# Attention and MLP interleaved in one pipeline over 384-token tiles

## The chip, the cores and the metric

The kernel runs on one core of one Trainium2 chip. A core has a matrix engine (PE, with its weight loads listed as PEld), a vector engine (DVE), an activation engine (ACT), a general engine (POOL, which also issues DMAs) and a sync engine (SP, which here only issues DMAs). They run side by side, each through its own list of instructions in order, and wait for one another on semaphores. PE multiplies a stationary operand that it has loaded with a moving one and writes to PSUM, which has eight banks of 2 KB per partition; DVE and ACT read PSUM, POOL does not. The metric is the device time in microseconds.

## What is computed

Causal attention for 4 batch entries, 8 heads, 768 positions and head size 64, and behind it an MLP over the 3,072 rows of 512 (8 heads x 64):

```python
scores = scale * np.matmul(q, k.transpose(0, 1, 3, 2))
stream_keep = causal & (is_sink | in_win)   # sink: first 4 keys, window: last 64
mask = np.where(retr[0, :, 0, 0, None, None], full_mask, stream_mask)  # per head
scores = np.where(mask[None, :, :, :], scores, -1000000000.0)
...
a = a / (np.sum(a, axis=-1, keepdims=True) + 1e-09)
return np.matmul(a, v).astype(np.float32)
...
x = np.ascontiguousarray(attn_out.transpose(0, 2, 1, 3)).reshape(B * S, H * D)
h = x @ w_in          # 512 -> 2048
g = h - np.tanh(h)
return (g @ w_out).astype(np.float32)
```

`is_retrieval` is read at run time; a retrieval head sees all earlier keys, a streaming head the sink and the window. Inputs and output are fp32; the products are taken in fp16 with fp32 sums.

## The kernel before

The kernel has two stages, one after the other. A framework gives each engine its list from the program, reordered by its own estimate of when operands are ready; buffers are handed round by tags with a number of buffers each.

**Start.** POOL issues everything that is loaded: q and k of two batch entries in blocks of 128 positions (`load_qk`, lines 84 and 88, 128 KB each), cast from fp32 to fp16 by the DMA, then v (line 96) and the whole of w_in (line 118). Then POOL makes small patterns and DVE writes them into `R01` and `S01` and, for each head, one mask `hmask` over all of its 21 causal blocks (line 188, 128 x 2,688).

**Attention** goes by unit `u`, a pair of heads (`hp`) of one batch entry, 16 units. `emit_transposes` (lines 215 and 219) turns q and k blocks with PE against an identity, and ACT copies them to `qk` (line 223). For each chunk of up to 512 columns PE makes the scores of both heads (`sc`, line 259; each uses 64 of the 128 rows), ACT takes the exp into `pt` (line 267). DVE multiplies the whole `pt` of a head with its mask (line 276). For each of six query blocks PE sums `av` over the key blocks (line 281; v has a column of ones, so column 64 is the row sum), DVE takes the reciprocal (line 289) and scales into `x` (line 290, 64 columns). After the four head pairs of a batch entry PE transposes `x` (line 303) and DVE copies it to `xT` (line 310). PSUM: four banks for `sc`, two for `tp` and `xtp`, two for `av`.

**MLP**, when all of `xT` is there, goes by 8 tiles of 384 rows. For each of 16 blocks `fb` PE sums four matmuls into `ph` (line 328), ACT takes tanh into `th` (line 336), and DVE makes `gt` (line 337). Then, for each 128 rows, PE sums 16 matmuls of 512 columns into `po` (line 344), ACT copies it to `ot` (line 352), and SP stores it. PSUM: four banks for `ph`, two for `po`.

## Time and profile before

| | before |
|---|---|
| median of 3 runs (lowest, highest) | 431.13 us (430.26, 431.20) |
| span of the profiled execution | 429.8 us |
| busy: PE, PEld | 357.2 us, 175.1 us |
| busy: DVE, ACT, POOL | 245.9 us, 209.6 us, 60.5 us |

The span runs from the first to the last instruction of the one execution that was profiled; the runs are timed without a profile, and their median stands 1.3 us above it. In the profile a line such as L281 is the kernel's line 281, an arrow `out<-in` names the tiles, and in the groups the three parts behind it are: count, busy time with the mean of one instruction in ns, and the engine's idle time ahead of them with what ended it. A busy PE is not PE at its peak, since matmuls are pipelined and each one's duration holds its latency.

### The profile page before, as it was taken

The page shows a single profiled execution, that of the slowest core. Times are in us where ns is not written, and L with a number is a line of the kernel's source. Part 1 is how long each engine was busy: PE and PEld are TensorE (multiplying, and loading weights), DVE is VectorE, ACT ScalarE, POOL GpSimd, SP SyncE. Part 2 cuts the span into 40 slices and gives each one's busy share as a digit, 9 for nine tenths or more (in the row PEclk, how much of TensorE's full clock was granted, in tenths as well). Part 3 has the DMA queues.
Part 4 walks back from the last instruction along what each step waited for, and adds up shares of the span by engine and source line. Part 5 has one row for each costly group of instructions (what it writes and reads, how often), then busy time and mean ns, then how long its engine had stood idle before and what let it go on. Part 6 is the DMA issues. An engine that isn't in the chain of part 4 may idle for free.

```text
span 429.8 us, 5768 instructions
## 1 busy us (share of the span) xinstructions
PE 357.2 (83%) x2112; PEld 175.1 (41%) x2112; DVE 245.9 (57%) x676; ACT 209.6 (49%) x505; POOL 60.5 (14%) x71
## 2 busy tenths in 40 slices
PE   1694000888999999999998679999999999999996
PEld 0332000433354334543343335454545454545552
DVE  0005999678767769578767886261707080717160
ACT  1594000666568665776566305262717262635351
POOL 9948801000227011000000000000000000000000
PEclk9999999999999999999999999999999999999999
DMA  9999993800789009000000000101010101020201
GB/s 89 149 142 197 139 67 54 142 2 0 50 34 139 2 2 74 2 0 2 0 2 0 2 0 2 50 26 50 26 49 26 49 24 61 14 75 0 75 0 73
DMA packets 80779, 20.29 MB, mean 47 GB/s; under 512 B 75120, under 2 KB 77168, under 8 KB 80752
## 3 DMA queue, kind: packets, MB, share of 16 engines
q0 software_dynamic: 77152, 13.63, 43.0%
q1 hardware_dynamic: 3600, 6.30, 3.9%
q8 instruction: 16, 0.26, 0.2%
q14 instruction: 11, 0.09, 0.1%
HBM read 27.27 MB, written 6.29 MB: 78 GB/s over the span
## 4 chain that ended last, share of the span: by engine, by line
PE 71%; DVE 15%; POOL 5%; issue 3%; ACT 3%; DMA 3%; POOLq 0%; ACTq 0%
PE ph L328 20%; PE po L344 19%; PE sc L259 14%; PE av L281 11%; DVE hmask L188 4%; DVE pt L276 4%; PE xtp L303 3%; DMA v<-in_v_dram 3%; POOL qraw L84 2%; POOL kraw L88 2%; DVE x L290 2%; PE tp L215 2%; ACT pt L267 2%; DVE xT L310 1%; DVE rinv L289 1%
## 5 line engine op out<-in xcount | busy, mean ns | idle before, releaser
L267 ACT ACTIVATE pt<-sc 128x512 f16<-128x512 f32 (+3 forms) x256 | 103.2, 464 | 75.0 <-PE av L281 46.8
L337 DVE SCALAR_TENSOR_TENSOR gt<-th,ph 128x384 f16<-128x384 f32 x128 | 71.0, 554 | 88.5 <-ACT th L336 77.3
L281 PE MATMUL av<-v,pt 128*128 128x65 f16 x672 | 70.3, 243 | 45.7 <-DVE pt L276 32.5
L259 PE MATMUL sc<-qk 64*128 64x512 f16 (+3 forms) x256 | 92.4, 454 | 5.4 <-ACT pt L267 3.0
L328 PE MATMUL ph<-xT,w_in_t 128*128 128x384 f16 x512 | 86.9, 332 | 0.4 <-DVE xT L310 0.4
L344 PE MATMUL po<-w_out_t,gt 128*128 128x512 f16 x384 | 84.2, 379 | 0.0
L336 ACT ACTIVATE th<-ph 128x384 f32<-128x384 f32 x128 | 62.7, 490 | 39.2 <-PE ph L328 39.2
L281 PEld LDWEIGHTS <-pt 128*128 128x128 f16 x672 | 43.7, 123 | 92.1 <-DVE pt L276 32.8
L328 PEld LDWEIGHTS <-w_in_t 128*128 128x128 f16 x512 | 50.8, 99 | 36.2 <-issue 3.4
L290 DVE TENSOR_SCALAR x<-av,rinv 128x64 f16<-128x64 f32 x192 | 53.2, 281 | 4.3
L344 PEld LDWEIGHTS <-gt 128*128 128x128 f16 x384 | 37.6, 98 | 44.5
L289 DVE RECIPROCAL rinv<-av 128x1 f32<-128x1 f32 x192 | 31.1, 165 | 36.9 <-PE av L281 35.2
L276 DVE TENSOR_TENSOR pt<-pt,hmask 128x2688 f16<-128x2688 f16 x32 | 49.3, 1542 | 0.0
L223 ACT CAST qk<-tp 128x256 f16<-128x256 f32 x96 | 32.9, 382 | 32.0 <-PE tp L219 31.7
L352 ACT ACTIVATE ot<-po 128x512 f32<-128x512 f32 x24 | 14.3, 597 | 69.8 <-PE po L344 69.8
L215 PE MATMUL tp<-ident,qraw 128*128 128x128 f16 x96 | 25.7, 287 | 10.3 <-DMA qraw<-in_q_dram 7.1
L259 PEld LDWEIGHTS <-qk 64*128 64x128 f16 x256 | 19.6, 102 | 29.2 <-issue 17.0
L219 PE MATMUL tp<-ident,kraw 128*128 128x128 f16 x96 | 27.3, 311 | 4.2 <-DMA kraw<-in_k_dram 4.2
L310 DVE CAST xT<-xtp 128x128 f16<-128x128 f32 x96 | 25.3, 285 | 4.6 <-PE xtp L303 3.2
L303 PE MATMUL xtp<-ident,x 128*128 128x128 f16 x96 | 24.1, 278 | 2.5 <-DVE xT L310 1.5
L188 DVE SCALAR_TENSOR_TENSOR hmask<-R,retr_f,S 128x2688 f16<-128x2688 f16 x8 | 23.5, 3015 | 0.0
L84 POOL DMA_DIRECT2D qraw<-in_q_dram x24 | 22.8, 949 | 4.5 <-PE av L281 4.1
(34 smaller groups left out, 88.7 us busy)
## 6 DMA issues: line engine op xcount, KB each, us to landing
out_dram<-ot SPq DMA_DIRECT2D x24, 256.0 KB, 2.0
qraw<-in_q_dram POOLq DMA_DIRECT2D x24, 128.0 KB, 4.7
kraw<-in_k_dram POOLq DMA_DIRECT2D x24, 128.0 KB, 4.7
v<-in_v_dram POOLq DMA_DIRECT2D x4, 768.0 KB, 10.4
w_in_t<-in_moe_w_in_dram POOLq DMA_DIRECT2D x1, 2048.0 KB, 18.3
w_out_t<-in_moe_w_out_dram POOLq DMA_DIRECT2D x1, 2048.0 KB, 14.9
retr_i<-in_is_retrieval_dram SPq DMA_DIRECT2D x1, 8.0 KB, 2.5
```

The lines of the kernel that those rows point to most:

```text
L188: nc.vector.scalar_tensor_tensor(out=hmask[h][:], in0=R01[:], scalar=retr_f[:, 2 * h : 2 * h + 1], in1=S01[:], op0=ALU.mult, op1=ALU.add,)
L259: nc.tensor.matmul(out=pscs[hh][:, 0:cw], lhsT=qk[lo : lo + 64, S + jb * 128 : S + jb * 128 + 128], rhs=qk[lo : lo + 64, jb * 128 + c0 : j ...
L267: nc.scalar.activation(out=pts[hh][:, OFF[jb] + c0 : OFF[jb] + c0 + cw], in_=pscs[hh][:, 0:cw], func=AF.Exp, scale=inv_sqrt_d,)
L276: nc.vector.tensor_mul(out=pt[:], in0=pt[:], in1=hmask[h][:])
L281: nc.tensor.matmul(out=pav[:, 0 : D + 1], lhsT=pt[:, c0 : c0 + 128], rhs=v1[:, h, jb, :], start=(jb == 0), stop=(jb == qb),)
L289: nc.vector.reciprocal(out=rinv[:], in_=pav[:, D : D + 1])
L290: nc.vector.tensor_scalar(out=xts[b][qb][:, h * D : h * D + D], in0=pav[:, 0:D], scalar1=rinv[:], scalar2=XS, op0=ALU.mult, op1=ALU.mult,)
L303: nc.tensor.matmul(out=px[:], lhsT=xts[b][qb][:, cb * 128 : cb * 128 + 128], rhs=ident16[:], start=True, stop=True,)
L328: nc.tensor.matmul(out=ph[:], lhsT=w_in_t[:, cb, fb * 128 : fb * 128 + 128], rhs=xT[cb][:, tt * TTN : tt * TTN + TTN], start=(cb == 0), st ...
L336: nc.scalar.activation(out=th[:], in_=ph[:], func=AF.Tanh, scale=1.0 / XS)
L337: nc.vector.scalar_tensor_tensor(out=gt[:, fb, :], in0=th[:], scalar=-XS, in1=ph[:], op0=ALU.mult, op1=ALU.add,)
L344: nc.tensor.matmul(out=po[:], lhsT=gt[:, fb, tsub * 128 : tsub * 128 + 128], rhs=w_out_t[:, fb, :], start=(fb == 0), stop=(fb == NFB - 1),)
```

## The change

The kernel is written anew around 8 tiles of 384 positions, two per batch entry: `t` is the tile, `c = t % 2` its half. In the first half (even tiles) a head has 6 causal blocks, in the second (odd) 15. Line numbers of the new program stand in the rows below.

- **Loads.** SP loads q and k of a tile in fp32, each partition taking three neighbouring positions of a head (768 bytes), `load_qk`. `cast_qk` makes fp16 copies: on DVE for tiles 0 and 1, on POOL for the others. v comes in blocks of 128 positions, w_in and w_out in four parts each, all by POOL.
- **Transposes** (`st_T`): six per tile and head pair into one PSUM bank in fp16, and one DVE copy of 768 elements to `qkT`, which puts positions back in order. ACT has no part in it.
- **Scores and exp** (`st_S`): blocks are packed into groups of up to 512 columns per head, both heads in one PSUM tile of two banks, one exp for both.
- **Masks.** Only the diagonal block and the one before it are multiplied with a mask, `m4` (512 columns per head). Blocks farther away have no mask: they use `vf`, copies of v and its ones column multiplied with the head's flag (1 or 0) by POOL, `far_v`; in block 0 the sink rows keep theirs.
- **av** (`st_A`): all three query blocks and both heads of a tile in one PSUM bank, one reciprocal and one multiply of 384 elements. The scale 4,096 sits in the ones column as 1/4,096. `st_X` transposes the result into the same bank tag `m` (one bank), and one DVE copy makes `xT`.
- **Pipeline.** The program has 128 steps, one for each `fb` of the 8 tiles. A step is `H_unit` (the `ph` sum, tanh and `gt` of tile `t`), pieces of a later tile's attention by a table `plan`, and three `po` matmuls of tile `t - 1` (`O_mms`). Tile 0's attention stands ahead of the steps, tile 1's lies in steps 0 to 15, an even tile's later on in 9 steps and an odd one's in 23; steps 112 to 127 have none. Behind the steps come the 48 `po` matmuls of the last tile.
- **PSUM**: two tiles of two banks for `sc` and the transposes, one bank `m`, two for `ph` (`h`), one for `po` (`o`).

On DVE, at the start of the program, the rows before are (`R`, `sdiag`, `soff` are parts of the masks):

```order
L127 CAST retr_f<-retr_i 128x16
L106 CAST ident_90<-ident_85 128x128
L171 CAST R_144<-causal 128x128
L160 TENSOR_TENSOR sdiag<-causal,winlo 128x128
L162 TENSOR_TENSOR tmpm<-winlo,sinkrows 128x128
L166 TENSOR_TENSOR soff_162<-offwin,sinkrows 128x128
L164 TENSOR_TENSOR sdiag_160<-causal,tmpm 128x128
L171 CAST R_144<-causal 128x128 x5
```

And now, at the same place (`raw_q`, `raw_k` are the fp32 tiles, 97 and 99 of tile 0, 163 and 165 of tile 1; `t_q`, `t_k` their fp16 copies):

```order
L201 CAST t_q_149<-raw_q_97 128x1536
L201 CAST t_k_151<-raw_k_99 128x1536
L155 TENSOR_SCALAR nz<-retr_i 128x16
L160 TENSOR_TENSOR rflag<-nz 128x8
L201 CAST t_q_360<-raw_q_163 128x1536
L128 CAST ident_111<-ident_106 128x128
L201 CAST t_k_362<-raw_k_165 128x1536
L225 COPY qkT_0_175<-tp_176 128x2x3x128
L162 TENSOR_TENSOR rflag_134<-rflag,sinkrows 128x8
L168 TENSOR_TENSOR tmpm<-winlo,sinkrows 128x128
```

The casts of both tiles, and with them the wait for four loads, have moved ahead of the first copy of transposed q and k and of the masks.

On ACT, in the middle of attention, the rows before are (`pt_2156` and `pt_2157` belong to the two heads of a pair):

```order
L267 ACTIVATE pt_2156<-sc_2182 128x512
L267 ACTIVATE pt_2157<-sc_2183 128x512
L267 ACTIVATE pt_2156<-sc_2188 128x384
L267 ACTIVATE pt_2157<-sc_2189 128x384
L267 ACTIVATE pt_2156<-sc_2194 128x256
L267 ACTIVATE pt_2157<-sc_2195 128x256
```

And now, in the steps of tile 1 and the first of tile 2 (`th` is the tanh of a step, the number behind it `fb`; `ot` the eviction of `po`):

```order
L269 ACTIVATE pt_1171<-sc_2_1230 128x2x512
L269 ACTIVATE pt_1171<-sc_3_1235 128x2x384
L346 ACTIVATE th_12_1245<-ph_12_1240 128x384
L346 ACTIVATE th_13_1272<-ph_13_1267 128x384
L346 ACTIVATE th_14_1291<-ph_14_1286 128x384
L346 ACTIVATE th_15_1312<-ph_15_1307 128x384
L363 ACTIVATE ot_2_1318<-po_2_1198 128x512
L346 ACTIVATE th_0_1329<-ph_0_1324 128x384
L269 ACTIVATE pt_1336<-sc_0_1337 128x2x512
L269 ACTIVATE pt_1336<-sc_1_1342 128x2x512
L346 ACTIVATE th_1_1355<-ph_1_1350 128x384
```

The MLP's tanh and evictions have moved from behind all exps to between them, so that a tanh can now stand behind two exps of both heads.

The diff, cut to its core:

```diff
-        qraw = load_pool.tile([128, NSB, H, D], FP16, tag="qraw", name="qraw")
-        kraw = load_pool.tile([128, NSB, H, D], FP16, tag="kraw", name="kraw")
...
+    raw_pool = pool("raw", 4)
+    t16_pool = pool("t16", 2)
...
+    pt_pool = pool("pt", 3)
...
+    def load_qk(t):
+        b, c = divmod(t, 2)
+        for nm, src in (("q", q), ("k", k)):
+            r = raw_pool.tile([128, H, NB, D], FP32, tag="raw", name=f"raw_{nm}{t}")
+            nc.sync.dma_start(
+                out=r[:].rearrange("p h i d -> p h (i d)"),
+                in_=src[b, :, c * TT : (c + 1) * TT, :].rearrange(
+                    "h (p i) d -> p h (i d)", i=NB
+                ),
+            )
...
+    def mask_head(h):
+        nc.vector.scalar_tensor_tensor(
+            out=m4[:, h, :], in0=D4[:].rearrange("p a c -> p (a c)"),
+            scalar=rflag[:, h : h + 1], in1=S4[:].rearrange("p a c -> p (a c)"),
+            op0=ALU.mult, op1=ALU.add,
+        )
...
-        nc.vector.scalar_tensor_tensor(
-                out=hmask[h][:], in0=R01[:], scalar=retr_f[:, 2 * h : 2 * h + 1],
...
+    def far_v(t):
+        b, c = divmod(t, 2)
+        parts = ((0, 1, rflag0), (1, 3, rflag)) if c == 0 else ((3, 4, rflag),)
+        for lo, hi, fl in parts:
+            nc.gpsimd.tensor_mul(
+                out=vfs[b][:, :, lo:hi, :],
+                in0=v1s[b][:, :, lo:hi, :],
+                in1=fl[:].unsqueeze(2).unsqueeze(3).to_broadcast([128, H, hi - lo, D + 1]),
+            )
...
+    def cast_qk(t, eng):
+        for nm in ("q", "k"):
+            c16 = t16_pool.tile([128, NB, H, D], FP16, tag=f"t16{nm}", name=f"t16_{nm}{t}")
+            eng.tensor_copy(
+                out=c16[:], in_=raws[nm, t][:].rearrange("p h i d -> p i h d")
+            )
...
+        tp = bank([128, 2, NB, 128], FP16, "sc", 2, f"tp{n}")
+        for g, nm in enumerate(("q", "k")):
+            for i in range(NB):
+                nc.tensor.transpose(
+                    out=tp[:, g, i, :], in_=t16s[nm, t][:, i, 2 * hp : 2 * hp + 2, :],
+                    identity=ident16[:],
+                )
+        nc.vector.tensor_copy(
+            out=qkT[b, hp][:, :, c * TT : (c + 1) * TT].rearrange("x g (p i) -> x g i p", i=NB),
+            in_=tp[:],
+        )
...
+    GROUPS = {
+        0: [[(0, 0, 2), (1, 1, 2)], [(2, 2, 1), (0, 2, 1)]],
+        1: [[(3, 3, 2), (4, 4, 2)], [(5, 5, 1), (2, 3, 3)], [(0, 3, 3), (3, 5, 1)], [(1, 3, 3)]],
+    }
...
+            sc = bank([128, 2, 512], FP32, "sc", 2, f"sc{n}_{gi}")
+            o = 0
+            for jb, q0, nb in GROUPS[c][gi]:
+                for hh in range(2):
+                    lo = 64 * hh
+                    nc.tensor.matmul(
+                        out=sc[:, hh, o : o + nb * 128],
+                        lhsT=qk[lo : lo + 64, 1, jb * 128 : jb * 128 + 128],
+                        rhs=qk[lo : lo + 64, 0, q0 * 128 : (q0 + nb) * 128],
+                        start=True, stop=True,
+                    )
...
+            nc.scalar.activation(
+                out=pts[n][:, :, o0 : o0 + w], in_=sc[:, :, 0:w], func=AF.Exp, scale=inv_sqrt_d
+            )
...
-            nc.vector.tensor_mul(out=pt[:], in0=pt[:], in1=hmask[h][:])
+        if g0 == 0:
+            pt = pts[n]
+            hs = slice(2 * hp, 2 * hp + 2)
+            if c == 0:
+                nc.vector.tensor_mul(out=pt[:, :, 0:512], in0=pt[:, :, 0:512], in1=m4[:, hs, :])
+                nc.vector.tensor_mul(
+                    out=pt[:, :, 512:640], in0=pt[:, :, 512:640], in1=m4[:, hs, 256:384]
+                )
+            else:
+                pv = pt[:, :, 0:768].rearrange("p a (r c) -> p a r c", r=3)
+                nc.vector.tensor_mul(
+                    out=pv, in0=pv,
+                    in1=m4[:, hs, 256:512].unsqueeze(2).to_broadcast([128, 2, 3, 256]),
...
+            avs[n] = bank([128, NB, 2, D + 1], FP32, "m", 1, f"av{n}")
...
+                    vv = v1s[b] if jb >= qb - 1 else vfs[b]
+                    co = COL[c][jb, qb]
+                    nc.tensor.matmul(
+                        out=av[:, i, hh, :], lhsT=pts[n][:, hh, co : co + 128],
+                        rhs=vv[:, h, jb, :], start=(x == 0), stop=(x == len(order) - 1),
+                    )
...
-                rinv = sm_pool.tile([128, 1], FP32, tag="rinv")
...
+            rinv = sm_pool.tile([128, NB, 2], FP32, tag="rinv", name=f"rinv{n}")
+            nc.vector.reciprocal(out=rinv[:], in_=av[:, :, :, D])
+            x16 = x_pool.tile([128, NB, 2, D], FP16, tag="x16", name=f"x16_{n}")
+            nc.vector.tensor_mul(
+                out=x16[:], in0=av[:, :, :, 0:D],
+                in1=rinv[:].unsqueeze(3).to_broadcast([128, NB, 2, D]),
+            )
...
+        xp = bank([128, NB, 128], FP16, "m", 1, f"xp{n}")
+        for i in range(NB):
+            nc.tensor.transpose(
+                out=xp[:, i, :], in_=x16s[n][:, i, :, :], identity=ident16[:]
+            )
+        nc.vector.tensor_copy(out=xTs[t][:, hp, :], in_=xp[:].rearrange("p i c -> p (i c)"))
...
-    ps_h = ctx.enter_context(tc.tile_pool(name="ps_h", bufs=4, space=bass.MemoryType.PSUM))
-    ps_o = ctx.enter_context(tc.tile_pool(name="ps_o", bufs=2, space=bass.MemoryType.PSUM))
...
+        ph = bank([128, TT], FP32, "h", 2, f"ph{t}_{fb}")
...
+                pos[t] = bank([128, DM], FP32, "o", 1, f"po{t}_{ts}")
...
+        qa = [lambda: st_A(n, (0, 1), False), lambda: st_A(n, (2,), True)]
+        qs = quanta_S(nS) if nS is not None else []
+        res = []
+        while qs or qa:
+            if qs:
+                res.append(qs.pop(0))
+            if qa:
+                res.append(qa.pop(0))
+        if nT is not None:
+            res.append(lambda: st_T(nT))
+        res.append(lambda: st_X(n))
+        return res
+
...
+    NU = NTT * HP
+    cast_qk(0, nc.vector)
+    for h in range(H):
+        mask_head(h)
+    far_v(0)
+    load_qk(1)
+    load_v(1)
+    ones_v(1)
+    for j in (2, 3):
+        load_w_in(j)
+    st_T(0)
+    st_T(1)
...
+    def span(t):
+        if t == 1:
+            return 0.0, 16.0
+        lo = 16.0 * (2 * ((t - 2) // 2) + 1)
+        return (lo, lo + 9.0) if t % 2 == 0 else (lo + 9.0, lo + 32.0)
...
+    for t in range(1, NTT):
+        lo, hi = span(t)
+        fs = []
+        for hp in range(HP):
+            n = t * HP + hp
+            if first:
+                fs += [lambda: st_T(HP), lambda: st_T(HP + 1)] + quanta_S(HP)
+                first = False
+            if hp == 0 and t + 1 < NTT:
+                fs.append(lambda t=t: load_qk(t + 1))
+                fs.append(lambda t=t: (load_v(t + 1), ones_v(t + 1)))
+            if hp == 1 and t + 1 < NTT:
+                fs.append(lambda t=t: cast_qk(t + 1, nc.gpsimd))
+                fs.append(lambda t=t: far_v(t + 1))
+            fs += slot(n, n + 1 if n + 1 < NU else None, n + 2 if n + 2 < NU else None)
+        for i, f in enumerate(fs):
+            put(int(lo + (hi - lo) * i / len(fs)), f)
+
...
+    for t in range(NTT):
+        for fb in range(NFB):
+            s = t * NFB + fb
+            fs = plan.get(s, [])
+            half = (len(fs) + 1) // 2
+            for f in fs[:half]:
+                f()
+            H_unit(t, fb)
+            for f in fs[half:]:
+                f()
+            if t:
+                O_mms(t - 1, 3 * fb, 3 * fb + 3)
...
+    O_mms(NTT - 1, 0, NB * NFB)
```

More of the change, by code (lines that the diff above doesn't have):

```diff
@@ L92, in load_qk, with ones_v, load_w_in @@
-        loads[b] = (qraw, kraw)
-    def load_v(b):
-        v1 = v_pool.tile([128, H, NSB, D + 1], FP16, tag="v1", name="v1")
+                out=v1s[b][:, :, i, 0:D],
+                in_=v[b, :, i * 128 : (i + 1) * 128, :].rearrange("h p d -> p h d"),
+            )
+    def ones_v(t):
+        b, c = divmod(t, 2)
+        nc.gpsimd.memset(v1s[b][:, :, c * NB : (c + 1) * NB, D : D + 1], 1.0 / XS)
+    w_in_t = []
+    w_out_t = []
+    def load_w_in(j):
+        w = w_pool.tile([128, HP, 512], FP16, tag=f"win{j}", name=f"win{j}")
```

431 lines of the change are left out of this document (176 added, 255 removed).

## The prediction, made before the changed kernel had run

> **What bounds the kernel now.** I read the busy table by stretch first, then the chain of work that ended last, the groups of instructions by shape, the waits, and the timeline at the seams. The stretches (columns: length, then PE, weight loads, DVE, ACT, POOL busy):
>
> ```profile
> 0.00:40.00 40.00, 23.18 (x108) 9.93 (x108) 3.75 (x12) 23.89 (x69) 31.19 (x41) 1.00 1.85 143
> 40.00:70.00 30.00, 0.00 (x0) 0.00 (x0) 29.93 (x26) 0.00 (x0) 13.44 (x15) 1.00 1.38 90
> 70.00:257.00 187.00, 165.39 (x1108) 76.83 (x1109) 141.19 (x512) 108.68 (x284) 15.87 (x17) 1.00 0.38 29
> 257.00:425.80 168.80, 168.65 (x896) 88.31 (x895) 71.00 (x129) 76.45 (x151) 0.00 (x0) 1.00 0.10 37
> ```
>
> Three limits follow one another: 70 us of start, in which PE stands still from 40 to 70 while DVE builds masks; 187 us of attention; 169 us of MLP with PE full and DVE and ACT half idle.
>
> ```profile
> 1.36 1.00 POOL qraw L84
> ...
> 22.63 10.89 DMA v<-in_v_dram
> ...
> 53.91 14.73 DVE hmask L188 x5
> ...
> 257.08 12.97 PE ph L328 x64
> 270.05 10.36 PE po L344 x48
> 280.41 10.40 PE ph L328 x64
> ...
> 425.82 0.60 ACT ot L352
> ```
>
> The chain's start runs over POOL, which issues 24 loads of q and k, then v, then the masks' first steps behind them, and DVE's `hmask` last. In the MLP a `ph` matmul takes 10.40/64 = 0.1625 us, a `po` 10.36/48 = 0.216. The first tile's `ph` took 2.57 longer, in its first 16 matmuls:
>
> ```profile
> 257.08 5.17 PE L328 MATMUL ph<-xT,w_in_t 128*128 128x384 f16 x16 [0.38 <-DVE xT L310]
> ```
>
> That is 0.323 each, twice 0.1625: PE had come out of attention at half speed. The clock column reads 1.00 everywhere, so only durations show it. The groups by shape agree, 512 columns take 598 ns in attention (L259) and 379 in the MLP (L344):
>
> ```profile
> L344 PE MATMUL po<-w_out_t,gt 128*128 128x512 f16 x384 | 84.2, 379 | 0.0
> L337 DVE SCALAR_TENSOR_TENSOR gt<-th,ph 128x384 f16<-128x384 f32 x128 | 71.0, 554 | 88.5 <-ACT th L336 77.3
> L281 PE MATMUL av<-v,pt 128*128 128x65 f16 x672 | 70.3, 243 | 45.7 <-DVE pt L276 32.5 <-DVE x L290 12.4
> L336 ACT ACTIVATE th<-ph 128x384 f32<-128x384 f32 x128 | 62.7, 490 | 39.2 <-PE ph L328 39.2
> L267 ACT ACTIVATE pt<-sc 128x512 f16<-128x512 f32 x96 | 57.0, 612 | 56.9 <-PE av L281 46.8 <-DVE x L290 5.4 <-PE sc L259 4.0
> L290 DVE TENSOR_SCALAR x<-av,rinv 128x64 f16<-128x64 f32 x192 | 53.2, 281 | 4.3
> L259 PE MATMUL sc<-qk 64*128 64x512 f16 x96 | 51.5, 598 | 2.3 <-ACT pt L267 1.1 <-ACT qk L223 0.5
> ...
> L276 DVE TENSOR_TENSOR pt<-pt,hmask 128x2688 f16<-128x2688 f16 x32 | 49.3, 1542 | 0.0
> ...
> L289 DVE RECIPROCAL rinv<-av 128x1 f32<-128x1 f32 x192 | 31.1, 165 | 36.9 <-PE av L281 35.2
> ...
> L310 DVE CAST xT<-xtp 128x128 f16<-128x128 f32 x96 | 25.3, 285 | 4.6 <-PE xtp L303 3.2
> ...
> L188 DVE SCALAR_TENSOR_TENSOR hmask<-R,retr_f,S 128x2688 f16<-128x2688 f16 x8 | 23.5, 3015 | 0.0
> ...
> L267 ACT ACTIVATE pt<-sc 128x128 f16<-128x128 f32 x64 | 17.4, 296 | 5.9 <-PE sc L259 5.5
> ...
> L352 ACT ACTIVATE ot<-po 128x512 f32<-128x512 f32 x24 | 14.3, 597 | 69.8 <-PE po L344 69.8
> ```
>
> PE's weight loads in attention wait for DVE's many small evictions of `av`:
>
> ```profile
> PE av L281 <- DVE pt L276: 32.5, 1, 32.5
> ...
> PEld L281 <- DVE x L290: 30.2, 64, 3.1
> ...
> PEld L281 <- DVE rinv L289: 18.5, 55, 0.9
> ```
>
> **The change, part by part.**
>
> *DVE and ACT prices.* ACT: (612-296)/3 = 105 ns per 128 columns, so 1,024 columns take 1.03 us and 768 take 0.82. A head pair of an even ("light") tile has exps of 1,024 and 512: 1.65 us; of an odd ("heavy") tile three of 1,024 and one of 768: 3.92. DVE from PSUM: (554-285)/256 = 1.05 ns per element, so the `qkT` copy of 768 elements takes 0.96; `x16` and `xT` (384) 0.55 each by L337, the reciprocal 0.17 by L289. Masks by L276: 1,280 elements for a light pair (in two instructions: 0.73 in proportion, 1.06 if each adds L289's 165 ns as a fixed part; I take 0.9), 1,536 for a heavy one (0.88 to 1.05; 0.95). So DVE pays 3.13 for a light and 3.18 for a heavy pair, 6.3 for what took it 159/16 = 9.9 (L276, L289, L290, L310 over 16 head pairs of a whole batch entry), the `qkT` copies that it takes from ACT included.
>
> *PE prices.* Four transposes follow in 0.29 us, eleven `av` matmuls in 0.79, and two 512-column score matmuls of a head pair in 0.73, 0.13 apart, side by side:
>
> ```profile
> 22.93 0.29 PE L215 MATMUL tp<-ident,qraw 128*128 128x128 f16 x1
> ...
> 23.22 0.31 PE L219 MATMUL tp<-ident,kraw 128*128 128x128 f16 x1
> ```
>
> ```profile
> 158.39 0.79 PE L281 MATMUL av<-v,pt 128*128 128x65 f16 x11
> ```
>
> ```profile
> 149.92 0.73 PE L259 MATMUL sc<-qk 64*128 64x512 f16 x2
> ```
>
> At half speed a transpose costs 0.10, an `av` (0.79-0.24)/10 = 0.055 (the last one's own 0.24 is L281's mean), a score pair 0.84 ns a column (0.323/384). At full speed: transpose 0.05, score pair 0.42 ns; `av`, never seen there, between 0.027 and 0.055, I take 0.04. Light pair: 9 transposes, 768 paired columns, 12 `av` = 0.45+0.33+0.48 = 1.26 us (half speed 2.2). Heavy: 0.45+0.81+1.20 = 2.46 (4.15). Not side by side, scores add 0.33 and 0.81. A step is one H unit (4 x 0.1625) and three `po` (3 x 0.216): 1.30 us.
>
> *A, start.* POOL's 24 q,k issues and the 23.5 us of `hmask` go; m4 costs 8 x 3.015 x 512/2,688 = 4.6, say 5.2 with fixed parts. What is late next is q,k itself, in fp32 on SP's queue, beside v and w_in on POOL's:
>
> ```profile
> q0 software_dynamic: 77152, 13.63, 43.0%
> q1 hardware_dynamic: 3600, 6.30, 3.9%
> ...
> retr_i<-in_is_retrieval_dram SPq DMA_DIRECT2D x1, 8.0 KB, 2.5
> ```
>
> A packet took 0.43 x 16 x 429.8/77,152 = 38 ns (256 B read) or 75 ns (mean 1.75 KB). A tensor of one tile is 1,024 packets of 768 B, between those: 2.4 to 4.8 us. In DVE's order the casts of tile 1 stand ahead of the first `qkT` copy, so four tensors must land: 10 to 19 us, 3 more for the issue and the 2.5 of latency that `retr_i` shows, and up to 8 where v's 3 x 1,024 packets of 38 ns come between on the same 16 engines; 13 to 30, taken 20. Then cast 1.3 (0.85 to 1.7, at half or all of 1.05 ns), two copies 1.9, ten small ones 2.5, m4 5.2, masks 0.9: first `av` at 32, against
>
> ```profile
> 70.17 0.35 PE L281 MATMUL av<-v,pt 128*128 128x65 f16 x3 [32.54 <-DVE pt L276]
> ```
>
> Tile 0's four pairs then run one behind the other through the single bank `m`: `av` 0.9, reciprocal 0.2, a `qkT` copy 0.96 and a mask 0.9 between, `x16` 0.55, transposes 0.55, `xT` 0.55 = 4.6. MLP starts at 32+18 = **50** (it was 257).
>
> *B, steps 0 to 15* (H of tile 0, heavy tile 1, no `po` due): PE 16 x 0.65 + 4 x 2.46 = 20 at full speed, 37 at half; ACT 16 x 0.49 + 15.7 = 23.5; DVE 16 x 0.554 + 12.7 = 21.6. PE begins at half speed, is then full, and should rise: **28** (24 to 37).
>
> *C, steps 16 to 111*, three times a light tile over 9 steps and a heavy one over 23. PE 32 x 1.30 + 4 x 1.26 + 4 x 2.46 = 56.5 (x3 = 169); DVE 32 x 0.554 + 25.2 = 43 (129); ACT 32 x 0.49 + 22.3 + 6 x 0.6 = 41.6 (125). So MLP work covers nearly all of attention's DVE and ACT time. Not covered, by my estimate: a light tile's 9 steps hold 9 x 0.554 + 4 x 3.13 = 17.5 of DVE against 9 x 1.30 + 4 x 1.26 = 16.7 of PE, about 3 with hand-overs (x3 = 9). A tanh behind two exps gives its `h` bank back after 0.33 + 2.06 + 0.49 + 0.55 = 3.4, while PE has two `po` groups, an H unit and 18 `av` to do, 3.0: 0.4 per heavy pair (x12 = 5). The single `o` bank comes back after 0.4 of latency and 0.6 of eviction, behind 0.65 of H: 0.3 x 18 = 5. **188**, with 170 if all is hidden.
>
> *D, steps 112 to 127*: 16 x 1.30 + 3 x 0.45 = **22**. *E, the last 48 `po`*: 10.4, two bank waits of 1.1, and the 4.0 us that now lie between 425.82 and the span's end: **16.6**.
>
> Out-stores, w_in, w_out and v cost nothing: their queues stand nearly idle after 70 us, and POOL's 32 issues of about 1.0 us (the chain's first row) fall in 250 us. If q,k or a cast came late, a tile's 9 or 23 steps stand ahead of it; with that cover gone, the next `qkT` copy waits on DVE, and with it the `gt` behind it and PE's `h` banks. The flag-scaled copies of V take the far blocks out of DVE's mask multiplies (2,688 elements per head and batch fall to 1,408) and put `far_v` on POOL, which is busy 16 of 187 us there: at nothing, while DVE has its slack; without it, the second rival.
>
> Sum 50+28+188+22+16.6 = 304.6 of span. The profiled span is 429.8, the median 431.13, so 1.3 lie around it: **306 us**.
>
> **Rivals.**
>
> That MLP and attention are not interleaved at all is excluded by ACT's order above.
>
> *The clock stays low (slower than before).* Speaks for it: 187 us of attention, PE 88% busy by the table, never rose. Against: there PE waited for `av` evictions; here it is short of time in B at half speed (37 against 23.5). If it held through B and C: C = 3 x (32 x 2.59 + 4 x 2.2 + 4 x 4.15) = 325, total 306+137+9 = 452. It decides the sign from (431-306-9)/137 = 85% of C on; half of C gives 384. The Trainium skill ("TensorE: Matmul & The Clock Gate", "A second HAM failure mode: psum-queue depth-cycling") has this as a rule against such a change: a PE that cycles through PSUM banks with short idle gaps swings between both clocks. By that rule, the half-and-half time is the one to expect; the attention rows bear out the low clock, no row a swing.
>
> *DVE and POOL block each other.*
>
> ```profile
> 37.24 2.33 POOL L169 MEMSET S<- 128x2688 f16 x1
> ...
> 37.77 2.72 DVE L171 CAST R<-causal 128x128 f16<-128x128 f32 x5
> ```
>
> Five casts of 128 elements, 0.7 us in all at 1.05 ns an element, took 2.72: they began beside the memset and ended after it. A cast of 1,536 elements at the memset's 0.87 ns would take 1.3 us, say 1.5 with a read. If each of POOL's 17 operations in C (10 casts, 7 `far_v`) held DVE so long where DVE is the limit, C grows by 25: 331. Against: heavy stretches have 14 us of DVE slack each.
>
> *Everything hides*: `av` at 0.027 (pairs of 1.10 and 2.07, C at 163), the first `av` at 25: 306-25-7 = 274.
>
> **Chances.** Forecast 0.60 (288 to 325); low clock through C 0.04 (452), in a part of it 0.10 (330 to 430); DVE held 0.14 (325 to 346); all hidden 0.12 (270 to 288). The range 278 to 346 leaves out about 0.2. Faster by over 0.2% (what can be told from no change) 0.95; within 0.01; slower 0.04.
>
> **What would show it.** `ph` at 326 to 332 ns and `po` at 379 from about 60 us on (524 and 600: low clock); first `av` near 32; `ph` from 50; PE idle under 25 us in C, ended by DVE `gt` and `xT`; POOL casts beside stretched mask multiplies. Wrong if PE idles over 15% of C, or if the casts of tile 1 come after 30.

## The result, and the profile after

The changed kernel takes **310.14 us** (median; runs of 309.1 to 310.9) against 431.16 beside it on the same chip: ratio 0.720, 95% interval 0.718 to 0.721. The profiled execution took 309.1 and spans 307.4. Here and below a median takes in every run of a kernel, while a ratio leaves out a run more than 1.5% above the kernel's fastest (there was one in e_maskall and one in e_nat).

The busy table by stretch, cut at the first `av`, the fifth `ph` matmul (the first on the third head pair's `xT`), the starts of steps 16 and 112, and the end of the last `ph` (columns as before: length, then PE, weight loads, DVE, ACT, POOL busy, the clock, DMA):

```profile
0.00:34.29 34.29, 4.07 (x35) 2.80 (x35) 19.74 (x29) 4.31 (x5) 13.35 (x24) 1.00 1.19 236
34.29:49.22 14.93, 10.18 (x104) 6.68 (x105) 11.78 (x20) 4.47 (x6) 8.49 (x10) 0.99 1.28 204
49.22:79.93 30.71, 28.50 (x294) 15.71 (x292) 22.75 (x40) 21.83 (x33) 14.73 (x15) 0.89 0.87 139
79.93:268.34 188.41, 175.52 (x1623) 98.19 (x1622) 124.35 (x225) 112.32 (x183) 29.31 (x27) 1.00 0.25 49
268.34:289.37 21.03, 20.76 (x111) 10.73 (x110) 8.86 (x16) 8.91 (x19) 0.00 (x0) 1.00 0.10 38
289.37:307.40 18.03, 11.49 (x51) 4.78 (x49) 0.55 (x1) 2.88 (x5) 0.00 (x0) 1.00 0.15 59
```

Where the kernel before had 187 us of attention and then 169 of MLP, there is now one stretch of 188 in which PE works 175.5 and DVE and ACT 124 and 112. PE's idle time there is 12.9 us (188.4 less 175.5). The groups of that stretch (80 to 268) say what ended it; behind the last bar stand a group's idle time and what ended it:

```profile
L341 PE MATMUL ph<-xT,win 128*128 128x384 f16 x384 | 80.5, 326 | 0.5 <-DVE gt L347 0.5
L356 PE MATMUL po<-wout,gt 128*128 128x512 f16 x276 | 77.8, 379 | 1.8 <-ACT ot L363 1.8
L259 PE MATMUL sc<-qkT 64*128 64x128 f16 (+2 forms) x252 | 20.1, 268 | 5.9 <-DVE qkT L225 5.2 <-ACT pt L269 0.7
L324 PE MATMUL xp<-ident,x 128*128 128x128 f16 x72 | 8.0, 220 | 4.4 <-DVE x L311 4.3
```

`ph` and `po` have the durations of full speed. The clock row of the page shows one dip, in the seventh and eighth slice (a fall to half from 48.9 to 55.7 us); ahead of 45 us nothing is recorded, and durations there are those of half speed:

```profile
PEclk9999996899999999999999999999999999999999
```

The page's chain by line, and the two copies from PSUM among DVE's groups:

```profile
PE po L356 20%; PE ph L341 18%; DVE qkT L225 11%; PE sc L259 7%; ACT pt L269 6%; DMA raw_k<-in_k_dram 5%; PE av L303 4%; DVE gt L347 3%; DVE pt L276 3%; DVE x L311 3%; DVE pt L277 2%; ACT th L346 2%; ACT ot L363 2%; PE tp L221 2%; DVE m L180 1%
```

```profile
L225 DVE COPY qkT<-tp 128x768 f16<-128x768 f16 x32 | 45.9, 1434 | 1.4 <-PE tp L221 1.3
...
L327 DVE COPY xT<-xp 128x384 f16<-128x384 f16 x32 | 10.9, 342 | 2.0 <-PE xp L324 2.0
```

The largest line that is not PE's is the `qkT` copy: 11% of the chain, 1.43 us each. The copy of half as many elements, L327, takes a quarter of that.

The start, in DVE's timeline (time, length, what):

```profile
5.81 1.75 DVE L201 CAST t_q<-raw_q 128x1536 f16<-128x1536 f32 x1 [5.81 <-DMA raw_q<-in_q_dram]
8.50 1.75 DVE L201 CAST t_k<-raw_k 128x1536 f16<-128x1536 f32 x1 [0.94 <-DMA raw_k<-in_k_dram]
...
13.88 1.75 DVE L201 CAST t_q<-raw_q 128x1536 f16<-128x1536 f32 x1 [3.33 <-DMA raw_q<-in_q_dram]
15.54 0.22 DVE L128 CAST ident<-ident 128x128 f16<-128x128 f32 x1
20.20 1.75 DVE L201 CAST t_k<-raw_k 128x1536 f16<-128x1536 f32 x1 [4.43 <-DMA raw_k<-in_k_dram]
21.86 1.42 DVE L225 COPY qkT<-tp 128x768 f16<-128x768 f16 x1
```

Tile 0's q and k were cast by 10.25, but the identity (made at 5.4) stood behind tile 1's q, and the first `qkT` copy behind tile 1's k, for which DVE waited 4.43 us.

### The profile page after: what moved, and what is told of

It is laid out like the page before. It is cut to its first block, busy times and chain, and to the rows that moved or that the text cites. A ratio compares the mean times of both kernels' runs of the same rounds, so it can differ in the third digit from the quotient of the medians.

```text
span 307.4 us, 5361 instructions
## 1 busy us (share of the span) xinstructions
PE 250.5 (81%) x2208; PEld 138.9 (45%) x2208; DVE 188.0 (61%) x329; ACT 154.7 (50%) x249; POOL 65.9 (21%) x75
## 4 chain that ended last, share of the span: by engine, by line
PE 51%; DVE 26%; ACT 10%; DMA 5%; issue 5%; SPq 1%; ACTq 0%
PE po L356 20%; PE ph L341 18%; DVE qkT L225 11%; PE sc L259 7%; ACT pt L269 6%; DMA raw_k<-in_k_dram 5%; PE av L303 4%; DVE gt L347 3%; DVE pt L276 3%; DVE x L311 3%; DVE pt L277 2%; ACT th L346 2%; ACT ot L363 2%; PE tp L221 2%; DVE m L180 1%
## 5 line engine op out<-in xcount | busy, mean ns | idle before, releaser
L269 ACT ACTIVATE pt<-sc 128x1024 f16<-128x1024 f32 x96 | 82.8, 918 | 64.1 <-PE sc L259 63.8
L341 PE MATMUL ph<-xT,win 128*128 128x384 f16 x512 | 109.3, 331 | 0.5 <-DVE gt L347 0.5
L356 PE MATMUL po<-wout,gt 128*128 128x512 f16 x384 | 105.3, 379 | 4.2 <-ACT ot L363 4.0
L347 DVE SCALAR_TENSOR_TENSOR gt<-th,ph 128x384 f16<-128x384 f32 x128 | 69.1, 546 | 51.3 <-ACT th L346 51.0
L341 PEld LDWEIGHTS <-win 128*128 128x128 f16 x512 | 45.1, 99 | 30.8 <-issue 6.5
L259 PE MATMUL sc<-qkT 64*128 64x128 f16 (+2 forms) x352 | 32.0, 282 | 22.8 <-DVE qkT L225 15.0
L225 DVE COPY qkT<-tp 128x768 f16<-128x768 f16 x32 | 45.9, 1434 | 1.4 <-PE tp L221 1.3
L303 PEld LDWEIGHTS <-pt 128*128 128x128 f16 x672 | 29.0, 100 | 14.6 <-DVE pt L276 3.3
L259 PEld LDWEIGHTS <-qkT 64*128 64x128 f16 x352 | 14.4, 96 | 46.7 <-DVE qkT L225 19.2
L303 PE MATMUL av<-v,pt 128*128 128x65 f16 x352 | 28.8, 199 | 3.3 <-DVE pt L276 3.0
L95 POOL DMA_DIRECT2D v<-in_v_dram x24 | 21.7, 919 | 18.3 <-PE av L303 17.5
L303 PE MATMUL av<-vf,pt 128*128 128x65 f16 x320 | 24.0, 196 | 0.2
L311 DVE TENSOR_TENSOR x<-av,rinv 128x384 f16<-128x384 f32 x32 | 17.7, 552 | 0.7
## 6 DMA issues: line engine op xcount, KB each, us to landing
win<-in_moe_w_in_dram POOLq DMA_DIRECT2D x4, 512.0 KB, 14.6
```

The costliest lines, as they stand in the source:

```text
L95: nc.gpsimd.dma_start(out=v1s[b][:, :, i, 0:D], in_=v[b, :, i * 128 : (i + 1) * 128, :].rearrange("h p d -> p h d"),)
L225: nc.vector.tensor_copy(out=qkT[b, hp][:, :, c * TT : (c + 1) * TT].rearrange("x g (p i) -> x g i p", i=NB), in_=tp[:],)
L259: nc.tensor.matmul(out=sc[:, hh, o : o + nb * 128], lhsT=qk[lo : lo + 64, 1, jb * 128 : jb * 128 + 128], rhs=qk[lo : lo + 64, 0, q0 * 128 ...
L269: nc.scalar.activation(out=pts[n][:, :, o0 : o0 + w], in_=sc[:, :, 0:w], func=AF.Exp, scale=inv_sqrt_d)
L303: nc.tensor.matmul(out=av[:, i, hh, :], lhsT=pts[n][:, hh, co : co + 128], rhs=vv[:, h, jb, :], start=(x == 0), stop=(x == len(order) - 1),)
L311: nc.vector.tensor_mul(out=x16[:], in0=av[:, :, :, 0:D], in1=rinv[:].unsqueeze(3).to_broadcast([128, NB, 2, D]),)
```

## The experiments

All times are medians; ratios are to the kernel before, run beside them. Stage marks (us in the profiled span) of all kernels, worked out from the starts of the matmuls:

| kernel | time | ratio (95%) | first `av` | fifth `ph` | step 16 | step 112 | end of span |
|---|---|---|---|---|---|---|---|
| changed kernel | 310.14 | 0.718–0.721 | 34.3 | 49.2 | 79.9 | 268.3 | 307.4 |
| e_serial | 390.88 | 0.902–0.909 | 32.4 | 203.4 | 221.0 | 347.1 | 386.2 |
| e_start | 300.03 | 0.694–0.697 | 24.5 | 39.8 | 71.2 | 258.6 | 297.7 |
| e_readstride | 299.72 | 0.693–0.702 | 34.4 | 46.7 | 77.4 | 258.9 | 297.9 |
| e_contig | 295.13 | 0.681–0.687 | 33.0 | 42.9 | 69.1 | 253.7 | 292.8 |
| e_span | 300.24 | 0.696–0.701 | 36.4 | 50.5 | 79.4 | 259.0 | 298.0 |
| e_actcast | 307.68 | 0.712–0.718 | 36.5 | 48.7 | 80.4 | 268.1 | 307.1 |
| e_maskall | 309.89 | 0.717–0.723 | 33.2 | 49.1 | 81.2 | 268.6 | 307.6 |
| e_dmacast | 297.58 | 0.688–0.696 | 24.2 | 39.6 | 68.9 | 258.8 | 297.4 |
| e_obank | 308.10 | 0.714–0.719 | 35.9 | 50.6 | 81.0 | 270.4 | 306.3 |
| e_nat | 283.88 | 0.653–0.662 | – | – | – | – | – |
| b_full | 278.46 | 0.645–0.651 | 15.5 | 29.7 | 62.7 | 241.3 | 276.8 |
| b_two | 285.82 | 0.663–0.667 | 15.4 | 29.1 | 70.8 | 247.9 | 283.5 |

For e_serial the fifth column gives the first `ph`, which there comes behind all of attention. e_nat's profiled execution took 287.08, 3.2 us more than its median, so its marks are left out. Kernels with the same start differ at the first `av` by 2 us and more (34.3 to 36.5; 32.4 in e_serial), so a difference of 2 us between two rows' marks alone says little.

### Each part of the change undone

**e_serial**, the interleaving:

```diff
-            put(int(lo + (hi - lo) * i / len(fs)), f)
+            f()                       # attention of all tiles at once
...
+    with tc.issue_after(last attention transpose):
     for t in range(NTT):              # then the MLP of all tiles
```

> All of the changed kernel's attention runs first and its MLP after it (every H matmul is queued behind the last attention transpose; xT gets 8 buffers, ot 2). Theory (the MLP's PE work hides attention, and that is the larger part of the gain): attention alone is a chain through DVE, ACT and the single bank m. Tile 0's pairs followed each other every 4.6 us in the changed kernel (xT at 37.91, 42.49); at 4.6 for a light and 5.0 for a heavy pair 32 pairs take 154 from 34 on, the MLP then 169 plus 4.5 of tail, so 355 to 372 us, ph begins at about 190, and PE stays at half speed through attention. Rival (the lighter attention is the gain, interleaving adds little): pairs at DVE's own 3.5 and ACT's 3.9 make 118, MLP from 152, 322 to 330 us, with the clock up during attention.

It took 390.88: slower than either theory gave, on the side of the first. Attention ran from 32.4 to 203.4, pairs of heavy tiles 5.5 us apart (`x` at 188.66, 194.12, 199.63) where 5.0 was expected, and the MLP took 183 more, where the kernel before needed 173. PE at work and waiting, by stretch, the clock (no record stands ahead of 72 us, and durations there are those of half speed), and PE's largest wait over the whole run (us in all, times, longest):

```profile
32.42:203.40 170.98, 116.98 (x1279) 74.72 (x1280) 107.52 (x172) 80.79 (x92) 52.17 (x51) 0.70 0.50 74
203.40:368.14 164.74, 162.29 (x848) 83.32 (x847) 70.72 (x128) 72.27 (x147) 0.00 (x0) 0.98 0.09 33
```

```profile
PEclk9999999955656555655796999999999999999999
```

```profile
PE sc L260 <- DVE qkT L226: 48.0, 31, 5.7
```

So the 121 us of the change part into 40 (431 to 391) for everything else in it, and 81 (391 to 310) for interleaving. The 40 are nearly all the start: the first `av` moved from 70.17 to 32.4. The lighter attention by itself won 16 us (187 to 171), of which the MLP gave back 10. Lighter steps do little in a chain in which each engine waits for the next; what they did was to fit under the MLP. Of PE's 54 us of idle time in that stretch (171 less 117), 43.5 were score matmuls waiting for the `qkT` copy, which stands behind the reciprocal and `x16` in DVE's list. So the 81 us hold for this program with its stepped copy and its one bank `m`; a version with attention first that has a faster copy, or that gives attention the banks of the MLP, was not run, and might leave interleaving less to win.

**e_maskall**, the flag-scaled copies of V:

```diff
-                    vv = v1s[b] if jb >= qb - 1 else vfs[b]
+                    vv = v1s[b]
...
+                    nc.vector.tensor_scalar(   # far blocks, per head and flag
+                        out=pts[n][:, hh, lo:hi], in0=pts[n][:, hh, lo:hi],
+                        scalar1=fl[:, h : h + 1], scalar2=None, op0=ALU.mult,
+                    )
```

> The flag-scaled copies of V go; DVE multiplies the far key blocks by the head's flag in place (two instructions per light pair, six per heavy pair). By the multiplies' 0.28 us for 256 and 0.68 for 1,024 elements that is 0.42 us more per light and 2.1 more per heavy pair: 40 us more on DVE, and POOL's 12 multiplies of 1.05 to 2.0 go. Theory (in the heavy stretches DVE has 17 of 41 us free, so only the light tiles and tile 1 pay): 311 to 316 us. Rival 1 (the copies are what keeps DVE off the limit): 322 or more. Rival 2 (POOL's multiplies cost as much as they save, in the start and beside the masks): 305 to 309.

309.89, the same as with the copies. DVE's group of the new multiplies:

```profile
L299 DVE TENSOR_SCALAR pt<-pt,rflag 128x256 f16<-128x256 f16 (+3 forms) x128 | 33.8, 313 | 8.1 <-ACT pt L274 7.5
```

33.8 us more on DVE, and no time: heavy stretches grew (steps 25 to 48 from 41.4 to 43.4, 57 to 80 from 41.4 to 43.0), light ones shrank (48 to 57 from 24.2 to 20.7). In steps 48 to 57 of the changed kernel three mask multiplies had been stretched by 3.1 us beside POOL's `far_v`, which is gone here. Under the interleaving this part of the change is worth nothing measurable. The time lies between the first theory's range and the second rival's. The theory had the place wrong, since it let the heavy stretches go free and the light ones pay; the rival's mechanism shows.

**e_dmacast**, the fp32 loads with casts on chip (here undone, so that the DMA casts again):

```diff
-            nc.sync.dma_start(out=r[:].rearrange(...), in_=...)   # fp32, 768 B
+            for i in range(NB):
+                nc.gpsimd.dma_start(out=r[:, i, :, :], in_=...)   # to fp16, 256 B
```

> q and k come as fp16 by casting DMAs on POOL's queue, three per tensor and tile in 256-byte reads, and the sixteen casts on DVE and POOL go; positions are placed as in the changed kernel. Theory (fp32 loads on SP's queue buy the start): 6 x 1,024 packets of 38 ns on 16 engines take 15 us, v comes behind them on the same queue, first av at 34 to 42, and POOL's 36 more issues are hidden later while 17 us of its casts go: 308 to 320 us. Rival (the casts and the wait for tile 1's tensors cost more than small packets): first av under 32, 298 to 307.

297.58: the rival, and more. This part of the change **cost** 12.6 us. The 15 us that I had given to the small packets were too many: transposes began at 10.94, released by the identity, with all of tile 0's q and k there, and the first `av` stood at 24.2 instead of 34.3. From step 16 to 112 both kernels take about the same (190.0 and 188.4), so it is the start that differs, and the next kernel says by what.

**e_start**: the loads and casts stay; tile 1's casts are queued later.

```diff
-    cast_qk(1, nc.vector)
+    with tc.issue_after(xmul[1].ins):     # x16 of tile 0's second pair
+        cast_qk(1, nc.vector)
```

> Tile 1's two casts are queued on DVE behind the x16 of tile 0's second pair; nothing else is touched. Theory (the start waits in DVE's order for data that tile 0 does not need): ident is cast at 10.4 instead of 15.5, the first qkT copy stands at 11 instead of 21.9, the first av comes at 22 to 24 instead of 34.3, and 3.5 us come back as the casts now stand between tile 0's pairs: 300 to 304 us. Rival (the transfers set the start: v landed at 14.3, far_v follows on POOL and slows DVE, and the loads collide): first av at 29 or later, 306 to 311 us.

300.03, as the theory had it. The first `av`:

```profile
24.49 0.51 PE L304 MATMUL av<-v,pt 128*128 128x65 f16 x6 [4.64 <-DVE pt L277]
```

10 of the 12.6 us of the fp32 loads were the place of two casts in DVE's list, ahead of work that did not need them.

### The terms of the sum

**e_readstride** and **e_contig**, the `qkT` copy. The copy puts positions 3p+i in order, so it writes 2-byte elements 6 bytes apart.

```diff
-            out=qkT[...].rearrange("x g (p i) -> x g i p", i=NB), in_=tp[:],
+            out=qkT[...].rearrange("x g (p i) -> x g p i", i=NB),      # e_readstride
+            in_=tp[:].rearrange("x g i p -> x g p i"),
+            out=qkT[...], in_=tp[:].rearrange("x g i p -> x g (i p)"), # e_contig
```

> The qkT copy walks its elements in the order of the destination: it reads PSUM in steps and writes SBUF in order. Theory (the 1,434 ns are the 6-byte steps of 2-byte writes, and a copy in order goes at xT's 342 ns for 384): 0.62 to 0.75 us a copy, 32 x 0.75 = 24 us less DVE work, of it 4 to 5 in the start's chain and 5 to 8 in the light stretches: 298 to 302 us. Rival (stepping costs the same on the reading side, or the copy's cost is its element count from PSUM): 1.3 to 1.5 us a copy, 309 to 311 us.

> The qkT copy writes in the order in which it reads; the positions within a tile are left in the order of the transposes, so this kernel leaves out putting them back. It prices the step alone. Theory (the step costs): 0.62 to 0.65 us a copy, 297 to 301 us, DVE's waits ahead of score matmuls halved. Rival (768 elements from PSUM cost 1.4 us in any order): no change.

The groups of L225 in the two (e_readstride first):

```profile
L225 DVE COPY qkT<-tp 128x768 f16<-128x768 f16 x32 | 30.4, 949 | 0.8 <-PE tp L221 0.7
```

```profile
L225 DVE COPY qkT<-tp 128x768 f16<-128x768 f16 x32 | 17.5, 549 | 0.5 <-PE tp L221 0.4
```

The same 768 elements take 1,434 ns written in steps, 949 read in steps, 549 in order both ways. e_readstride's copy was slower than its theory (620 to 750) and its time, 299.72, fell into the theory's range all the same; e_contig, at 295.13, went below its own by 2 us. Of e_contig's 14.6 us of span, 10.8 were gained before step 16 and 3.8 after: the copy stands in tile 0's and tile 1's chains, where nothing covers it, and in the light tiles; under the heavy ones it cost nothing (41.3, 41.3 and 39.5 us against 41.4, 41.4 and 39.5). Not all of the 10.8 need be the copy's, since the changed kernel's profiled execution had 6.8 us at half clock in that part and e_contig's had none. The Trainium skill ("VectorE: DVE Perf Modes", "Mode 2×_1P — pack two bf16 into one 32-bit read") has the half-time of copies in order: two 16-bit values per cycle if they stand side by side. The runs agree: from 384 to 768 elements in order, 207 ns more (342 to 549), 0.54 ns each beside a fixed 135; with the same fixed part, reading in steps costs 1.06 an element ((949-135)/768), twice that. Writing in steps costs 1.69; no run shows why.

**e_span**, the spread of light tiles:

```diff
-        return (lo, lo + 9.0) if t % 2 == 0 else (lo + 9.0, lo + 32.0)
+        return (lo, lo + 12.0) if t % 2 == 0 else (lo + 12.0, lo + 32.0)
```

> A light tile's attention is spread over 12 steps and a heavy one's over 20 (they were 9 and 23). Theory (light stretches are short of DVE, heavy ones of PE, so PE work moved into the light ones fills their gaps): the three light stretches of the changed kernel held 66 us with 57 of PE busy; 9 us of idle shrink to 2 to 4, the heavy ones (PE busy 40 of 41) lose 3 steps and no more: 302 to 306 us. Rival (the gaps are single hand-overs through bank m and the qkT copy, as many per tile whatever the spread): 309 to 312 us.

300.24, a little more than the theory gave. Steps 16 to 112 take 179.5 instead of 188.4, with 6.2 us of PE idle instead of 12.9 (179.5 less 173.35 busy). So the light stretches were short of cover, and two numbers in the code gave back 10 us. PE's waits for `x16` and the `qkT` copy, 9.5 us there in the changed kernel, came down to 4.2.

**e_obank**, the single output bank, for the last two tiles only:

```diff
-                pos[t] = bank([128, DM], FP32, "o", 1, ...)
+                pos[t] = bank([128, DM], FP32, "m" if t >= NTT - 2 and ts % 2 else "o", 1, ...)
```

> For the last two tiles every second output group accumulates in the bank of tag m, which attention has left by then, instead of the single bank o. Theory (the single bank makes PE wait about 0.69 us at each of the last three groups, less in the steps before): 2 to 3 us less, 307 to 308.5. Rival (the end is set by the last group's eviction and store, and a wait that goes is found again there): 309.5 to 310.5.

308.10, as the theory had it. The intervals of the two kernels overlap slightly, but the place is the right one: from step 112 to the end it takes 35.9 us instead of 39.1. The end of PE's timeline in the changed kernel, two rows, and the same place here, one row without a wait:

```profile
295.00 3.61 PE L356 MATMUL po<-wout,gt 128*128 128x512 f16 x16 [0.69 <-ACT ot L363]
...
299.30 3.61 PE L356 MATMUL po<-wout,gt 128*128 128x512 f16 x16 [0.69 <-ACT ot L363]
```

```profile
290.67 11.17 PE L356 MATMUL po<-wout,gt 128*128 128x512 f16 x51
```

**e_actcast**, POOL against DVE:

```diff
-                fs.append(lambda t=t: cast_qk(t + 1, nc.gpsimd))
+                fs.append(lambda t=t: cast_qk(t + 1, nc.scalar))
```

> The twelve casts of tiles 2 to 7 run on ACT, not POOL; far_v stays on POOL. Theory (POOL slows only the mask multiplies beside it; in the changed kernel 7 of 48 were stretched, by 6.7 us in all): about half of the 6.7 goes, 307 to 309.5 us, and ACT's 12 x 1.3 us lie in its slack. Rival 1 of the prediction's kind (POOL's operations hold DVE 1.5 us each where DVE is the limit): 12 x 1.5 = 18 us less, 292 to 298. Rival 2 (a cast ahead of an exp or a tanh delays PE): 311 to 316.

307.68, about 2.5 less; its interval touches that of the changed kernel, and the two profiled spans are alike (307.1 and 307.4), so the size is uncertain, but 12 to 18 us are excluded. What a collision is shows in the changed kernel's timelines, POOL's and DVE's:

```profile
43.36 1.66 POOL L201 CAST t_q<-raw_q 128x1536 f16<-128x1536 f32 x1
```

```profile
43.63 1.55 DVE L277 TENSOR_TENSOR pt<-pt,m 128x256 f16<-128x256 f16 x1
```

A multiply that takes 0.28 alone ended 0.16 us after POOL's cast. After 34 us this happened to 7 of 48 mask multiplies, for 6.7 us in all; of the other groups (`gt`, `x16`, `xT`, the reciprocal, `qkT`, each with a PSUM input) no instruction was more than a quarter over its median.

### Together

**e_nat** joins e_dmacast with blocks of 128 positions, so that the copy may write in order:

```diff
-  in_=src[b, :, c * TT : (c + 1) * TT, :].rearrange("h (p i) d -> i p h d", i=NB)[i]
+  in_=src[b, :, c * TT + i * 128 : c * TT + (i + 1) * 128, :].rearrange("h p d -> p h d")
```

> Casting loads of q and k on POOL's queue as before, but with positions in blocks of 128 as the kernel before had them, so that the qkT copy writes in order and nothing needs putting back. Theory (the start's order and the stepped copy are separate costs): the casting loads alone gave 297.6, the copy in order took 15 us off, of it 6 ahead of the MLP's start, 4.5 in tile 1 and 4 later: 282 to 287 us. Rival (both take the same waits away): 290 to 296.

283.88, in the theory's range: the costs are separate.

**b_full** adds e_span and e_obank, and reorders the start:

```diff
+    with tc.issue_after(last_sel[0].ins):   # POOL: masks first
         load_v(0); load_w_in(0); load_w_in(1); ones_v(0)
...
-    for h in range(H):
-        mask_head(h)
+    mask_head(0); mask_head(1)              # the others just ahead of their pair
```

> The casting loads in blocks of 128 and the copy in order, with light tiles over 12 steps, the second output bank for the last two tiles, POOL's masks issued ahead of v and w_in, and the masks of heads 0 and 1 ahead of the others. Theory (four separate causes): from 284 for the first pair, the spread takes 5 to 7 more (its 10 us share the light stretches with the copy), the bank 2, the start 4 to 6: 270 to 277 us. Rival (PE's own 246 us busy, a start of 24 and a tail of 4.5 leave little to take): 278 to 284.

278.46, the best of all: 0.90 of the changed kernel, 0.648 of the kernel before. It fell into the rival's range, 1.5 us above the theory's: steps 16 to 112 take 178.5 with 175.3 of PE busy, so little is left there, but the stretch from the fifth `ph` to step 16, tile 1's, grew to 33.0 (30.7 in the changed kernel). In it PE waited 3.15 us for w_out's load, and later stand a DVE mask multiply, POOL's `far_v` beside it, and PE's wait for the `gt` behind:

```profile
39.17 0.38 PE L350 MATMUL po<-wout,gt 128*128 128x512 f16 x1 [3.15 <-DMA wout<-in_moe_w_out_dram]
```

```profile
56.60 3.77 DVE L270 TENSOR_TENSOR pt<-pt,m 128x1024 f16<-128x1024 f16 x1 [0.82 <-ACT pt L263]
```

```profile
56.85 2.95 POOL L188 TENSOR_TENSOR vf<-v,rflag 128x520 f16<-128x520 f16 x2
```

```profile
61.15 1.12 PE L335 MATMUL ph<-xT,win 128*128 128x384 f16 x3 [3.18 <-DVE gt L341]
```

The last three rows are the prediction's second rival in full, 3.2 us, once. About the end of each of the two waits PE's clock fell to half for 3.4 us (from 40.4 and from 60.9); why it fell is not shown.

**b_two** takes `far_v` to DVE to end that, and asks for w_out and the second half of w_in earlier (core of the edit):

```diff
-            nc.gpsimd.tensor_mul(out=vfs[b]...
+            nc.vector.tensor_mul(out=vfs[b]...
...
     load_v(1)
+    for j in range(4):
+        load_w_out(j)
     ones_v(1)
```

> The combined version with two more edits: far_v runs on DVE, so that POOL computes nothing beside DVE's mask multiplies, and w_in's second half and w_out are asked for ahead of POOL's memset that waits for v. Theory (in the combined version PE waited 3.2 us for gt, queued on DVE behind a mask multiply that far_v on POOL had stretched, 3.1 us for w_out, and the first masks were stretched by 3 us): 7 to 9 us less, 269 to 273 us. Rival (the DVE work of far_v, 12 x 0.5 to 1.1 us, and transfers that crowd the start give it back): 276 to 280.

285.82, 7.4 slower than b_full, so worse than the rival too. DVE's timeline and PE's:

```profile
53.15 1.85 DVE L188 TENSOR_TENSOR vf<-v,rflag 128x520 f16<-128x520 f16 x2 [9.31 <-POOL v L100]
```

```profile
55.52 2.40 PE L335 MATMUL ph<-xT,win 128*128 128x384 f16 x7 [9.73 <-DVE gt L341]
```

The next batch's v landed late, behind w_out; on POOL only `far_v` had waited for it, on DVE every `gt` behind it did, and PE with them. The earlier loads are not what cost: POOL's memset that waits for this v stands at 52.91 here and at 55.73 in b_full. The work was cheap (0.88 us a piece on average); the place in an ordered list was not. The version left untried is b_full with `far_v` on DVE placed a tile later.

## Why the prediction was right, point by point

The sum was 306.0, the time 310.14. By its steps:

- **A, the start** (first `av` 32, MLP at 50): the first `av` stood at 34.3. The four pairs that the sum counts end with tile 0's last `xT`, at 51.7, so they took 17.4 us, forecast 18; the mark at 49.2 in the tables is the third pair's and not this point. The last of the four tensors was cast at 20.20, forecast 20, and for the forecast's reason. The 2.3 us come from the `qkT` copies (two at 1.42, not 0.96), the cast (1.75, not 1.3) and DVE's small mask steps, two of which took 1.08 and 1.94 beside POOL's `far_v` (3.02 from 23.46). What I did not ask was what the wait for tile 1 was worth if taken out: 10 us, by e_start.
- **B** (28): from the last `xT` to step 16 it was 28.2 (the tables' 30.7 starts at the earlier mark). PE did rise to full speed, at 45.5, and fell back once for 6.8 us, which is 3.4 us of work between half and full. What the fall cost is not shown: between the same points e_span, without a fall, took 26.8, and e_readstride, also without one, 28.6.
- **C** (188): 188.4, by errors that cancel. PE's own work was 175.5, not 169: counted from start to start of the single matmuls, a `ph` took 0.170 and a `po` 0.233 on average, not 0.1625 and 0.216, where they alternate with small matmuls (their medians are still 0.162 and 0.216, so the excess lies at single seams); the attention matmuls came to 45.8, forecast 44.6. The waits were 12.9, not 19. The light stretches' 9 us came out at 9.1 (20.63+24.20+21.26 less 57.0 of PE busy), though for a partly mis-sized reason: a light pair cost DVE 3.5 (0.69+0.28 masks, 0.19, 1.43, 0.55, 0.34), not 3.13; the `qkT` copy was 0.47 too low and `xT` 0.21 too high, both priced at fp32's 1.05 ns an element. The tanh behind two exps was forecast at 5 and waits for `gt` were 0.5; the single `o` bank was forecast at 5 and waits for `ot` were 1.8. Nothing took their place: PE's waits behind DVE's `qkT` copy and `x16` (5.2 and 4.3) are for 7.3 us the light stretches' term itself, and 2.2 behind the copy fell into the heavy stretches, where the sum had none. There PE idled 3.8 us in all, against the 10 of the two forecast waits, and that and the 6.5 by which PE's own work was larger nearly cancel. That this term came within 0.4 us is luck to that extent.
- **D** (22): 21.0. **E** (16.6): 18.0, with three bank waits of 0.69 where I had two of 1.1, and 4.5 of tail for 4.0.
- **V, stores and weights at nothing**: right, by e_maskall for V; and behind the first `av` no wait of PE in the changed kernel was ended by a load. It also means that the flag-scaled copies earned nothing, which I had put as "DVE has its slack" and not drawn the end from.
- **Low clock, rival 1**: wrong for this kernel, but not for its attention: in e_serial the clock went to full four times for 3.4 us and back to half for 14 to 38, then once for 13.7 us at the end of attention, and stayed up only from shortly behind the MLP's start on. The rule that I cited (the Trainium skill, "TensorE: Matmul & The Clock Gate", "A second HAM failure mode: psum-queue depth-cycling") describes that swing; this case's trace agrees with the swing where attention runs alone (what sets it off is not shown), and with the MLP's matmuls between there is one fall and no swing.
- **DVE and POOL, rival 2**: the mechanism was right, 1.5 us a piece too (1.27 at 43.63), but after 34 us it met 7 of DVE's multiplies where I had let all of 17 POOL operations collide, and its casts cost 2.5 us or less, not 18. The Trainium skill ("SBUF — State Buffer", "Who interferes with whom") narrows it: two SBUF inputs on DVE collide with a POOL instruction that reads SBUF. The trace agrees for the mask multiplies, but it shows more than this rule covers. The mask step that took 1.94 is a copy with one SBUF input; in e_maskall a multiply by the flag, also with one, took 1.32 at 57.63 beside POOL's cast, where its median is 0.28; and the casts of the prediction's row, with one input each, stood beside a memset, which has no input. Instructions with an input in PSUM were not stretched.
- **What would show it**: `ph` 326 and `po` 379, PE idle under 25 (12.9), stretched mask multiplies beside POOL's casts: seen. That PE's waits would be ended by `gt` and `xT` was wrong.

## What to carry to other kernels

When a change has several parts, price each against the version without it: here interleaving two stages was worth 81 us against the same steps one stage after the other, the flag-scaled copies of V nothing, and the new loads cost 12. In an in-order engine list ask of each instruction what it waits for and who stands behind it: two casts, and in the last version one small multiply, placed ahead of work that did not need their data, cost 10 and 7 us. Spread the short stage's work over enough of the long one that the covering engine is never the one that waits; the balance was two numbers in the code and 10 us.

## What the runs showed of the hardware

- A DVE copy of 768 fp16 elements from PSUM: 549 ns in order, 949 when it reads in steps of 256 bytes, 1,434 when it writes in steps of 6 bytes.
- DVE's fp16 multiply of two SBUF operands grew by about the time that POOL worked on SBUF beside it: 0.28 became 1.55 beside a cast of 1.66, 0.69 became 3.77 beside two multiplies of 2.95 in all. One SBUF input was enough for a copy (1.94) and for a multiply by a scalar (0.28 became 1.32). Instructions with a PSUM input were not touched.
- Attention's short matmuls alone (e_serial, PE busy in 117 of 171 us) raised the clock four times for 3.4 us, with 14 to 38 us at half speed behind each, and once for 13.7. With the MLP's matmuls between them it held from 55.7 us to the end of the changed kernel's matmuls.
- Casting loads on POOL's queue, in 256-byte reads, had tile 0's q and k in place by 10.9 us, about as early as fp32 loads in 768-byte reads and two casts (10.25).
